# Keeping the late modes' rows twice, so that one 128-column stationary serves both row halves of a batch

## The chip, the cores and the metric

One core of a Trainium2 chip. The metric is device time in microseconds (us) of that core, as the median of several executions. Executions of one kernel mostly agree within 0.3%, so a change of 1 us needs many of them. In the profiles PE is the matmul engine, PEld its weight loads (the weights of a matmul are its stationary operand), DVE, ACT and POOL are the vector, scalar and GpSimd engines, and SP issues the stores.

## The reference

```python
def _attn_ref(q, k, v):                       # q, k, v: 8 x 8 x 576 x 64
    q_p, k_p = phi(q), phi(k)                 # phi(x) = elu(x) + 1
    kv  = einsum('bhsd,bhse->bhde', k_p, v)
    z   = sum(k_p, axis=2)
    num = einsum('bhsd,bhde->bhse', q_p, kv)
    return num / (einsum('bhsd,bhd->bhs', q_p, z)[..., None] + 1e-6)

def _moe_ref(x, w_r, w_i, w_ch):              # x: 8 x 576 x 512, 64 modes
    X = rfft(x, axis=1)[:, :64]
    Y = X * (w_r + 1j * w_i)                  # a 512 x 512 product for each mode
    u = x + irfft(Y, n=576, axis=1)
    return u + maximum(u @ w_ch, 0.0)
```

The weights of the 64 modes, 134 MB as float32, are read once.

## The kernel before

After attention and the forward transform the kernel walks over 32 pairs of modes. For each pair it loads the weights (two buffers), makes the product P, evicts it and turns it with `picks`. Work of other stages is handed out in slots between the pairs, and filler matmuls (`keep_warm`, tile zl) hold PE's clock.

```python
    def mode_pair(p):
        w = w_get(p)                           # waits for the weights of pair p
        ...                                    # 16 matmuls into P
        st = evacuate(p, P)
        work_slot(p, "mid")
        picks(2 * p, st, 2)
        if p % 4 == 3:
            ...                                # modes from 32 on:
            pin(nc.vector.tensor_copy(out=YL[:, :, :, g, :], in_=mode_rows(yt_ps)))
        work_slot(p, "end")
        keep_warm(FILL.get(p, 0))
```

The form stage, in the slots after pairs 27 to 30, makes two things from the late modes' rows of each batch b: `z`, the rows times w_ch, and `yp`, the rows transposed. Both are wanted twice, in partitions 0 to 63 and 64 to 127, for the inverse transform of the two row halves in the tail.

```python
    def form_z(b):
        z_ps = bank(f"z{b}")
        for ec in range(NDC):                  # NDC = 4
            yt = YL[:, ec].rearrange("p k g b -> p (k g) b")[:, :, b]    # 64 columns
            for h in range(2):
                pin(nc.tensor.matmul(z_ps[HALVES[h], :], yt, wch16[:, ec, :], ...))
        pin(nc.scalar.copy(out=YZ[b][:, 1, :], in_=z_ps))
    # form_y: the same with nc.tensor.transpose(y_ps[HALVES[h], ec, :], yt, id16)
```

Behind the last weights comes a tail of about 33 us: the last modes, then for each pair of row tiles six or more matmuls into `acc`, ReLU on ACT, the addition on DVE and a store of 512 KB to HBM (the first eight stores are of single tiles, 256 KB).

Of the kernel before, what the change touches and what calls it, by code (L numbers as in the profile page):

```python
# [11 lines left out]
F16 = mybir.dt.float16  # L12
# [31 lines left out]
def kernel(  # L44
# [10 lines left out]
    nc = tc.nc  # L55

    B, H, S, Dh = q.shape
# [3 lines left out]
    NDC = D // 128  # L61
# [5 lines left out]
    NL = 8  # L67
    NE = NM - NL
    NF = NM // 2
# [8 lines left out]
    xpool = ctx.enter_context(tc.tile_pool(name="xpool", bufs=1, side="right"))  # L78
    wpool = ctx.enter_context(tc.tile_pool(name="wpool", bufs=1, side="right"))

    id16 = const.tile([128, 128], F16, name="id16")
    fwd_sb = const.tile([128, 5, 2 * NM], F16, name="fwd_sb")
    pick_sb = const.tile([128, 32], F16, name="pick_sb")
    wch16 = const.tile([128, NDC, D], F16, name="wch16")
# [13 lines left out]

    QW = 4 * NJ * NP
    q_tile = lambda name: xpool.tile([128, QW], F16, tag="qTE", bufs=B, name=name)  # L100
    kv_all = [xpool.tile([128, 2, 2, 65], F16, tag="kv", bufs=B, name=f"kv{b}") for b in range(B)]
    rd_all = [xpool.tile([128, 5, 2, 4], F32, tag="rd", bufs=B, name=f"rd{b}") for b in range(B)]

    W_KEEP = 2
    pin = tc.keep_in_program_order
    PIECES = (slice(0, 2), slice(2, 4), slice(4, 6), slice(6, 7), slice(7, 8))
    HALVES = [slice(0, 64), slice(64, 128)]

    LAST = NM // 2 - 1
# [297 lines left out]
    def w_get(p: int):  # L407
        if p not in w_in and p == LAST:
            w_load_last(wpool, "w", W_KEEP)
        elif p not in w_in:  # L410
            for half in range(2):
                w_load(p, half, wpool, "w", W_KEEP)
        return w_in[p]

    def keep_warm(n: int):

        for _ in range(n):
            pin(nc.tensor.matmul(last_ps[0], id16, wch16[:, 0, :]))  # L418
# [4 lines left out]
    def work_slot(p: int, name: str):  # L423
        for _ in range(slots.get((p, name), 0)):
            if work:
                work.pop(0)()

    def product(P, x, n: int, w, dc: int, n_dc: int):
        c = dc % NDC * 32
        pin(  # L430
            nc.tensor.matmul(  # L431
                P[c : c + n, :], x, w[:, dc, :],
                start=(dc < NDC), stop=(dc >= n_dc - NDC), tile_position=(0, c),
                skip_group_check=True,
            )
        )

    def set_diagonal(p: int):
        for h in range(2):
            src = xt_v[HALVES[h], :, :, :, p].rearrange("p c t b -> p c (t b)")  # L440
            pin(nc.vector.tensor_copy(out=xz[p % 2][HALVES[h], :, h, :], in_=src))  # L441

    def evacuate(p: int, P):
        st = ystage.tile([128, D], F16, tag="ystage", bufs=2, name=f"ys{p}")
        if p % 2 == 0:
            pin(nc.vector.tensor_copy(out=st, in_=P))  # L446
        else:
            pin(nc.scalar.copy(out=st, in_=P))  # L448
        return st

    def picks(kk: int, st, n: int):
        for ec in range(NDC):
            pin(
                nc.tensor.matmul(  # L454
                    yt_ps[:, ec, kk % 8 : kk % 8 + n, :].rearrange("p m n -> p (m n)"),
                    st[:, ec * 128 : ec * 128 + 128],
                    pick_sb[:, 0 : n * 2 * B],
                )
            )

    def mode_pair(p: int):
        nonlocal yt_ps
        w = w_get(p)
        if p % 4 == 0:
            yt_ps = psW.tile([128, NDC, 8, 2 * B], F32, tag="yt", bufs=1, name=f"yt{p // 4}")
        P = psW.tile([128, D], F32, tag="P", bufs=2, name=f"P{p}")
        for dc in range(NDW):
            product(P, xz[p % 2][:, dc].rearrange("p h n -> p (h n)"), 32, w, dc, NDW)
        if p + 1 < LAST:
            set_diagonal(p + 1)  # L470
# [4 lines that stand above are left out]
            kk = 2 * p + 1  # L475
            if kk < NF:
                pin(nc.vector.tensor_copy(out=YE_T[:, :, kk - 7 : kk + 1, :], in_=yt_ps))
            else:
                g = (kk - NF) // NL + 1
                pin(nc.vector.tensor_copy(out=YL[:, :, :, g, :], in_=mode_rows(yt_ps)))  # L480
        work_slot(p, "end")
        keep_warm(FILL.get(p, 0))

# [47 lines left out]


    n_early = n_keep + n_pre
    FILL = {**{p: 7 for p in range(18, 27)}, 27: 9, 28: 5, 29: 6, 30: 4}
    ystage = ctx.enter_context(tc.tile_pool(name="ystage", bufs=1, side="right"))
    inv_sb = ystage.tile([2 * NM, S], F16, name="inv_sb")
    inv2_sb = ystage.tile([128, S], F16, name="inv2_sb")
# [1 line left out]
    lead_sb = [ystage.tile([128, S], F16, name=f"lead{b}_sb") for b in range(N_LEAD)]  # L539
    nc.sync.dma_start(out=inv_sb, in_=inv_dr.ap())  # L540
    YE_T = ystage.tile([128, NDC, NF, 2 * B], F16, name="YE_T")
    YL = ystage.tile([128, NDC, 2 * NL, NF // NL, B], F16, name="YL")
    Y8 = ystage.tile([128, NDC, NL, 2 * B], F16, name="Y8")
    nc.vector.memset(YL[:, :, :, 0, :], 0.0)

    def mode_rows(ps):
        return ps.rearrange("p c m (t b) -> p c (m t) b", b=B)

    yt_ps = None
# [5 lines left out]
    for p in range(n_early):  # L555
        mode_pair(p)
# [14 lines left out]
    def x_of(t: int):  # L571
        if t < B * NJJ:
            return x_main[t // NJJ][:, t % NJJ, :]
        i = t - B * NJJ
        return x_tail[i // 2][:, i % 2, :]
# [10 lines left out]
    def bank(name: str, shape=(128, D), dtype=F32):  # L586
        return psB.tile(list(shape), dtype, tag="bank", bufs=4, name=name)
# [115 lines left out]
    def form_z(b: int):  # L703

        z_ps = bank(f"z{b}")
        for ec in range(NDC):
            yt = YL[:, ec].rearrange("p k g b -> p (k g) b")[:, :, b]
            for h in range(2):
                pin(
                    nc.tensor.matmul(  # L710
                        z_ps[HALVES[h], :], yt, wch16[:, ec, :],
                        start=(ec == 0), stop=(ec == NDC - 1), skip_group_check=True,
                    )
                )
        pin(nc.scalar.copy(out=YZ[b][:, 1, :], in_=z_ps))

    def form_y(b: int):

        y_ps = bank(f"yp{b}", [128, NDC, 128], F16)
        for ec in range(NDC):  # L720
            yt = YL[:, ec].rearrange("p k g b -> p (k g) b")[:, :, b]
            for h in range(2):
                pin(nc.tensor.transpose(y_ps[HALVES[h], ec, :], yt, id16))
        pin(nc.vector.tensor_copy(out=YZ[b][:, 0, :], in_=y_ps.rearrange("p c r -> p (c r)")))

    def fold_lead(t: int):
# [35 lines left out]
    for b in range(B):  # L762
        pairs += [(b * NJJ, b * NJJ + 1), (b * NJJ + 2, b * NJJ + 3)]
        if b % 4 == 3:
            k = b // 4
# [82 lines left out]
    for b in range(B):  # L848
        work.append(lambda b=b: form_z(b))
        work.append(lambda b=b: form_y(b))  # L850
        if b < N_LEAD:
            work += [lambda t=t: fold_lead(t) for t in range(b * NJJ, b * NJJ + NJJ)]
    n_form = len(work) - n_fold
    first_fold, first_form = NF // 2 - 1, NE // 2 - 1
    fold_pairs = first_form - first_fold

    def share(n_items: int, steps: list):
# [10 lines left out]
    )  # L868
    share(
        n_form,  # L870
        [((first_form, "end"), 6)]
        + [((p, h), 4) for p in range(first_form + 1, LAST - 1) for h in ("mid", "end")]
        + [((LAST - 1, "mid"), 2), ((LAST - 1, "end"), 1)],
    )

    def first_rows(n: int):
# [18 lines left out]
    for p in range(n_early, LAST):  # L895
        mode_pair(p)
# [6 lines left out]
    for n in range(N_PRE):  # L903
# [6 lines left out]
    y_ps = [  # L910
        psW.tile([128, NDC, 128], F16, tag="P", bufs=2, name=f"ypl{h}")[:, 0 : NDC // 2] for h in range(2)
    ]
    y0 = psW.tile([128, D], F32, tag="P", bufs=2, name="y0l")
    last_ps.append(z1_ps.rearrange("p c m n -> p (c m n)"))
    rows = [Y8[:, ec].rearrange("p m n -> p (m n)") for ec in range(NDC)]
# [6 lines left out]
    for h in range(2):  # L922
        for ec in range(NDC):
# [3 lines left out]
                    start=(ec == 0), stop=(ec == NDC - 1),  # L927
# [5 lines left out]
    for h, eng in enumerate((nc.sync, nc.gpsimd)):  # L933
        eng.dma_start(
            out=YZ_all[64 * h : 64 * h + 64 : NF // NL].rearrange("r b z d -> r b (z d)"),
            in_=last.rearrange("p z d -> p (z d)"),
# [15 lines left out]
    def sums_of(n: int, i: int):  # L952
# [8 lines left out]
            out=x_of(0), in0=accs[0][:, 0], scalar=0.0, in1=x_of(0), op0=ALU.max, op1=ALU.add  # L961
# [50 lines left out]
```

## Time and profile before

| | before |
|---|---|
| time, median of 6 | 421.37 us (421.16 to 421.89) |
| span of the profiled execution | 419.6 us |
| PE, DVE, ACT busy | 69%, 54%, 37% of the span |
| the chain's last wait for weights ends | 386.75 us |
| last store issued by | 414.7 us |

In the page's rows of slices each digit is a tenth; in the chain of work the columns are start, duration and what it was; in the table of windows they are named in its first line.

### The profile page before, as it was taken

To read this page: it belongs to the slowest core of one execution; us is meant where nothing else is said; L and a number is where in the kernel's file an instruction comes from. 1 tells how busy PE (TensorE), PEld (TensorE's weight loads), DVE (VectorE), ACT (ScalarE), POOL (GpSimd) and SP (SyncE) were. 2 spreads that over 40 slices of the span, in tenths; PEclk is the share of its full clock that TensorE was granted. 3 is DMA by queue.
4 is the path that set the end of the run, shared out by engine and by line. 5 is a ranking of instruction groups with operands and counts; after the bars stand their busy time and mean duration, and the time that the engine had idled before them with its cause. 6 is when DMAs were issued, how large, how long until landed. Compare 5 with 4: busy or idle time off the path is not lost.

```text
span 419.6 us, 7400 instructions
## 1 busy us (share of the span) xinstructions
PE 288.7 (69%) x3115; PEld 155.9 (37%) x3115; DVE 228.6 (54%) x499; ACT 154.2 (37%) x253; POOL 58.1 (14%) x100
## 2 busy tenths in 40 slices
PE   0359799899517553444343685998798878899993
PEld 0247677787301221222121232433343324354421
DVE  4587979994404462464645353454455433512794
ACT  4677888954101011000000233344253422230782
POOL 4222224210001111111111111111111111130000
PEclk9999958989655555555555589799899989999997
DMA  8999999999999999999999999999999999998698
GB/s 219 211 212 216 210 221 206 229 206 222 222 217 212 213 223 211 216 222 209 220 220 205 225 220 205 225 215 209 224 217 208 225 216 209 223 205 162 230 395 328
DMA packets 17073, 93.17 MB, mean 222 GB/s; under 512 B 2112, under 2 KB 3024, under 8 KB 12880
## 3 DMA queue, kind: packets, MB, share of 16 engines
q0 software_dynamic: 12496, 81.48, 93.3%
q1 hardware_dynamic: 4544, 11.22, 7.2%
q8 instruction: 24, 0.39, 0.3%
q14 instruction: 9, 0.07, 0.0%
HBM read 163.93 MB, written 9.44 MB: 413 GB/s over the span
## 4 chain that ended last, share of the span: by engine, by line
DMA 65%; PE 19%; DVE 5%; issue 3%; ACT 3%; POOL 2%; DVEq 0%; ACTq 0%; POOLq 0%
DMA w<-in_moe_w_i_dram 52%; DMA pick_sb<-row_pick 8%; PE P L431 7%; DMA k<-in_k_dram 5%; PE acc L747 3%; PE acc L787 2%; PE kvp L256 2%; ACT ke L207 2%; POOL w L116 2%; PE eps L688 1%; DVE x L292 1%; DVE ke L220 1%; POOL w L128 1%; DVE k L214 1%; PE zl L418 0%
## 5 line engine op out<-in xcount | busy, mean ns | idle before, releaser
L431 PE MATMUL P<-w,xz 128*32 128x512 bf16 x496 | 48.3, 530 | 64.3 <-DMA w<-in_moe_w_i_dram 61.8
L448 ACT CAST ys<-P 128x512 f16<-128x512 f32 x15 | 8.8, 585 | 131.6 <-PE P L431 131.6
L116 POOL DMA_DIRECT2D w<-in_moe_w_r_dram x31 | 17.8, 575 | 244.2 <-PE P L431 240.7
L431 PEld LDWEIGHTS <-xz 128*32 128x32 bf16 x496 | 13.2, 115 | 85.5 <-DMA w<-in_moe_w_i_dram 56.9
L446 DVE CAST ys<-P 128x512 f16<-128x512 f32 x17 | 11.8, 691 | 53.5 <-PE P L431 53.5
L688 PE MATMUL eps<-wch,xTw 128*128 128x512 f16 x144 | 40.6, 409 | 0.0
L162 PEld LDWEIGHTS <-qT 64*128 64x128 f16 (+1 forms) x640 | 22.8, 124 | 31.7 <-issue 17.2
L671 ACT CAST x16w<-x_main 128x512 f16<-128x512 f32 x32 | 19.8, 618 | 37.7 <-DVE x_main L669 37.7
L669 DVE TENSOR_TENSOR x_main<-ya,x_main 128x512 f32<-128x512 f32 x32 | 22.0, 691 | 18.7 <-PE ya L665 18.5
L256 PE MATMUL kvp<-vpad,ke 32*128 32x130 f16 x576 | 23.3, 255 | 9.1 <-ACT qT L243 6.4
L441 DVE COPY xz<-xt_c 64x256 bf16<-64x256 bf16 x62 | 22.9, 370 | 12.1 <-PE P L431 11.3
L696 ACT CAST E<-eps 128x512 f16<-128x512 f32 (+1 forms) x40 | 21.2, 539 | 19.5 <-PE eps L688 19.5
L256 PEld LDWEIGHTS <-ke 32*128 32x128 f16 x576 | 21.4, 113 | 10.8 <-issue 8.9
L162 PE MATMUL nw<-kv,qT 64*128 64x65 f16 (+1 forms) x320 | 18.9, 240 | 9.5 <-DVE x_tail L632 4.5
L418 PE MATMUL zl<-wch,id 128*128 128x512 f16 x93 | 23.0, 380 | 0.0
L292 DVE TENSOR_TENSOR x<-num,rd 128x512 f16<-128x512 f32 x32 | 22.1, 692 | 1.1
L236 PE MATMUL qTp<-id,qe 128*128 128x128 f16 x144 | 14.3, 278 | 11.7 <-DVE qe L220 9.5
L632 DVE TENSOR_TENSOR x_main<-nw,rd 128x256 f32<-128x256 f32 x32 | 11.2, 417 | 17.3 <-PE nw L162 17.3
L207 ACT ACTIVATE qe<-q 128x1152 f16<-128x1152 f16 (+1 forms) x16 | 17.9, 1157 | 7.5 <-DMA q<-in_q_dram 7.4
L454 PE MATMUL yt<-pick_sb,ys 128*128 128x32 f16 (+1 forms) x128 | 8.8, 186 | 16.9 <-DMA pick_sb<-row_pick 10.7
L680 DVE COPY xTw<-xTp 128x512 f16<-128x512 f16 x36 | 15.0, 416 | 10.0 <-PE xTp L678 9.9
L243 ACT COPY qT<-qTp 128x1152 f16<-128x1152 f16 x16 | 19.6, 1291 | 0.5 <-PE qTp L236 0.2
(118 smaller groups left out, 494.6 us busy)
## 6 DMA issues: line engine op xcount, KB each, us to landing
w<-in_moe_w_r_dram POOLq DMA_DIRECT2D x31, 1024.0 KB, 12.5
w<-in_moe_w_i_dram POOLq DMA_DIRECT2D x31, 1024.0 KB, 16.7
out_dram<-x_main SPq DMA_DIRECT2D x12, 512.0 KB, 3.8
k<-in_k_dram POOLq DMA_DIRECT2D x8, 576.0 KB, 13.1
v<-in_v_dram POOLq DMA_DIRECT2D x8, 576.0 KB, 14.4
q<-in_q_dram POOLq DMA_DIRECT2D x7, 576.0 KB, 12.8
out_dram<-x_main SPq DMA_DIRECT2D x8, 256.0 KB, 3.8
q<-in_q_dram SPq DMA_DIRECT2D x2, 576.0 KB, 4.5
```

What stands on the lines that cost most here:

```text
L116: nc.gpsimd.dma_start(out=w_in[p][half::2], in_=two.rearrange("g (r dc) e -> (g r) dc e", dc=NDW))
L162: mm = nc.tensor.matmul(num[hpo][orow, c0 : c0 + 65], qT[rows, hpp, h2, cols], kv_sb[rows, hpp, h2, :])
L207: pin(nc.scalar.activation(out=ev[:, c], in_=heads(nm, b, c), func=AF.Exp))
L256: nc.tensor.matmul(kv_ps[:, h2, 0:130], phi["k", b][r0 : r0 + 32, j // NJ, j % NJ].rearrange("p o d -> p (o d)"), vp[r0 : r0 + 32, :, j, 0 ...
L292: nc.vector.tensor_tensor(out=dst.rearrange("p (o c d) -> p o c d", o=2, c=4), in0=nv[:, :, :, 0:64], in1=rden.unsqueeze(3).broadcast_to([ ...
L418: pin(nc.tensor.matmul(last_ps[0], id16, wch16[:, 0, :]))
L431: nc.tensor.matmul(P[c : c + n, :], x, w[:, dc, :], start=(dc < NDC), stop=(dc >= n_dc - NDC), tile_position=(0, c), skip_group_check=True,)
L441: pin(nc.vector.tensor_copy(out=xz[p % 2][HALVES[h], :, h, :], in_=src))
L669: pin(nc.vector.tensor_tensor(out=x, in0=acc, in1=x, op=ALU.add))
L671: pin(nc.scalar.copy(out=x16w[t], in_=x))
L688: nc.tensor.matmul(e_ps, xT[:, c, :], wch16[:, c, :], start=(c == 0), stop=(c == NDC - 1))
L696: pin(nc.scalar.copy(out=dst, in_=e_ps[:, cols]))
```

## The change

The rows of the late modes are kept twice side by side, so that a single 128-column stationary writes both halves at once: eight matmuls become four, in z and in yp. The second copy takes the room of kv, which for that becomes one tile. The 24 items of the form stage are handed out sooner, so that pair 30 has none, and filler takes the room.

```diff
-    kv_all = [xpool.tile([128, 2, 2, 65], F16, tag="kv", bufs=B, name=f"kv{b}") for b in range(B)]
+    kv_sb = xpool.tile([128, B, 2, 2, 65], F16, tag="kv", bufs=1, name="kv_sb")
+    kv_all = [kv_sb[:, b] for b in range(B)]
@@
-                pin(nc.vector.tensor_copy(out=YL[:, :, :, g, :], in_=mode_rows(yt_ps)))
+                late_modes(g, yt_ps)      # two tiles YL0, YL1; 2 casts into each
@@
-    FILL = {**{p: 7 for p in range(18, 27)}, 27: 9, 28: 5, 29: 6, 30: 4}
+    FILL = {**{p: 7 for p in range(18, 27)}, 27: 7, 28: 10, 29: 12, 30: 10}
@@ (form_z; form_y in the same way)
-            for h in range(2):
-                pin(nc.tensor.matmul(z_ps[HALVES[h], :], yt, wch16[:, ec, :], ...))
+            pin(nc.tensor.matmul(z_ps, late_rows(ec, b), wch16[:, ec, :], ...))
@@ (share of the form stage's items)
-        [((first_form, "end"), 6)]
+        [((first_form, "end"), 8)]
         + [((p, h), 4) for p in range(first_form + 1, LAST - 1) for h in ("mid", "end")]
-        + [((LAST - 1, "mid"), 2), ((LAST - 1, "end"), 1)],
+        + [((LAST - 1, "mid"), 0), ((LAST - 1, "end"), 0)],
```

(`late_modes` makes YL1, clears two slots of zeros and casts; `late_rows` picks the 128 columns.)

More of the change, by code (lines that the diff above doesn't have):

```diff
@@ L541, with late_modes, late_rows @@
     YE_T = ystage.tile([128, NDC, NF, 2 * B], F16, name="YE_T")
-    YL = ystage.tile([128, NDC, 2 * NL, NF // NL, B], F16, name="YL")
+    YL = [ystage.tile([128, NDC // 2, 2, 2 * NL, NF // NL, B], F16, name="YL0")]
     Y8 = ystage.tile([128, NDC, NL, 2 * B], F16, name="Y8")
-    nc.vector.memset(YL[:, :, :, 0, :], 0.0)
+    def late_modes(g: int, ps):
+        if len(YL) == 1:
+            YL.append(
+                xpool.tile([128, NDC // 2, 2, 2 * NL, NF // NL, B], F16, tag="kv", bufs=1, name="YL1")
+            )
+            for yl in YL:
+                pin(nc.vector.memset(yl[:, :, :, :, 0, :], 0.0))
+        for h, yl in enumerate(YL):
+            rows = mode_rows(ps)[:, h * (NDC // 2) : h * (NDC // 2) + NDC // 2]
+            for d in range(2):
+                pin(nc.vector.tensor_copy(out=yl[:, :, d, :, g, :], in_=rows))
+    def late_rows(ec: int, b: int):
+        yl = YL[ec // (NDC // 2)][:, ec % (NDC // 2)]
+        return yl.rearrange("p d k g b -> p (d k g) b")[:, :, b]
     def mode_rows(ps):
@@ L706, in form_z @@
         for ec in range(NDC):
-            yt = YL[:, ec].rearrange("p k g b -> p (k g) b")[:, :, b]
-            for h in range(2):
-                pin(
-                    nc.tensor.matmul(
-                        z_ps[HALVES[h], :], yt, wch16[:, ec, :],
-                        start=(ec == 0), stop=(ec == NDC - 1), skip_group_check=True,
-                    )
+            pin(
+                nc.tensor.matmul(
+                    z_ps, late_rows(ec, b), wch16[:, ec, :], start=(ec == 0), stop=(ec == NDC - 1)
                 )
+            )
         pin(nc.scalar.copy(out=YZ[b][:, 1, :], in_=z_ps))
@@ L720, in form_y @@
         for ec in range(NDC):
-            yt = YL[:, ec].rearrange("p k g b -> p (k g) b")[:, :, b]
-            for h in range(2):
-                pin(nc.tensor.transpose(y_ps[HALVES[h], ec, :], yt, id16))
+            pin(nc.tensor.transpose(y_ps[:, ec, :], late_rows(ec, b), id16))
         pin(nc.vector.tensor_copy(out=YZ[b][:, 0, :], in_=y_ps.rearrange("p c r -> p (c r)")))
```

## The prediction

> **What bounds the kernel now.** I read the page's 40 slices first, then the chain of work that ended last, then a table of windows over the last 80 us, and last the timeline around the stage that is changed. Of the slices, three rows:
>
> ```profile
> PE   0359799899517553444343685998798878899993
> ...
> PEclk9999958989655555555555589799899989999997
> DMA  8999999999999999999999999999999999998698
> ```
>
> The transfers fill 90% or more of every slice but the first and three of the last four. PE is at 7 to 9 tenths too from slice 25 on (262 us), but part of that is filler: matmuls kept only to hold its clock, on tile zl. The chain says which of the two sets the time:
>
> ```profile
> 349.86 1.01 PE P L431 x16
> 350.87 0.29 issue
> 351.16 0.54 POOL w L116
> 351.69 16.66 DMA w<-in_moe_w_i_dram
> 368.39 1.08 PE P L431 x16
> 369.47 0.29 issue
> 369.76 2.15 POOL w L128 x4
> 371.91 14.79 DMA w<-in_moe_w_i_dram
> 386.75 0.36 PE y_last L512 x8
> ```
>
> Weights come in pairs of modes, into two buffers. The product P of pair 27 (349.86) frees a buffer, the load of pair 29 is issued, lands before 368.39, and so on to 386.75. One hop covers two pairs, 368.39 - 349.86 = 18.5 us (19.4 us in undisturbed hops, such as 173.21 to 192.63), so one load takes 9.7 us. While pair 29's load is issued, pair 28's is still in flight (pair 28 starts at 358.69): the queue holds about 358.7 - 352.2 = 6.5 us of work when the new issues are done. A P that comes a microsecond or two late therefore delays an issue, but not the stream. This is the point on which everything hangs. The windows show how near PE is to the stream's pace:
>
> ```profile
> core 0: us, PE busy (x) PEld busy (x) DVE busy (x) ACT busy (x) POOL busy (x), PEclk, DMA share, GB/s
> ...
> 349.80:358.70 8.90, 5.72 (x53) 2.96 (x52) 3.65 (x7) 1.17 (x2) 1.09 (x2) 1.00 1.02 217
> 358.70:368.40 9.70, 9.09 (x64) 4.17 (x65) 5.25 (x9) 3.51 (x6) 1.08 (x2) 1.00 1.02 216
> 368.40:378.10 9.70, 8.42 (x91) 5.90 (x91) 1.70 (x4) 2.93 (x5) 3.82 (x7) 1.00 0.96 203
> 378.10:386.70 8.60, 8.26 (x79) 3.92 (x79) 3.12 (x7) 0.58 (x1) 0.54 (x1) 1.00 0.90 179
> 386.70:400.00 13.30, 12.89 (x87) 5.63 (x87) 9.31 (x14) 8.95 (x18) 0.56 (x1) 1.00 0.66 224
> 400.00:413.00 13.00, 12.45 (x69) 3.15 (x68) 12.87 (x12) 11.12 (x21) 0.00 (x0) 1.00 1.02 402
> ```
>
> The form stage lies in the first four windows, all with transfers at 0.90 to 1.02 of full. After 386.7 follows a tail of about 33 us (inverse transform, ReLU, stores), in which no instruction is changed; its PE runs at the full clock (1.00). So the change can move the end in two ways only: by moving the landing of the last weights, or by moving the clock or the start of the tail.
>
> **What the Trainium skill says.** (1) "TensorE: Matmul & The Clock Gate", Part 3 (small-M matmuls): matmuls whose outputs lie in different column groups run beside each other. The trace agrees: each row of z is made by two 64-column matmuls, and eight of them, 379 ns each, take 1.14 us together, not the 1.7 us of eight in series. (2) "TensorEngine Tiling (Array Packing)", Restrictions: column tiling switches the fast weight load off. Agrees: a 128x64 load for yp has a median of 214 ns, a 128x128 load for xTp 98 ns. (3) "VectorE: DVE Perf Modes", Mode 2x_2P: a PSUM source has one read port, so there is no doubled rate. Agrees: the 128x512 cast to YL takes 691 ns; at the page's 0.96 GHz 512 elements are 533 ns, which leaves 158 ns fixed. (4) The first page, Part 1: an idle array falls back to half clock. Agrees: the 16 products of a pair take 1.93 us at about 0.5 clock and 1.05 us at 1.00.
>
> **The change, part by part.**
>
> *z, eight batches.* Eight 64-column matmuls become four of 128 columns. The halves ran side by side already, so this is four passes of 512 rows before and after, 4 x 0.215 = 0.86 us. An eps group (four 128-column matmuls of 512) shows the same: 1.03 us from first start to last end against 1.14. I book 0.05 us a batch.
>
> *yp, eight batches.* Eight transposes with slow loads take 0.57 to 0.69 us; four 128-column ones, as in xTp, take 0.40 us. That is 0.2 to 0.3 us a batch.
>
> Together some 0.26 us a batch: pair 29's sequence z, yp repeats each 1.34 us (369.83 to 371.17), and four eps plus four xTp passes are 4 x 0.215 + 4 x 0.056 = 1.08 us. Times 8: PE gains 2.1 us, all of it inside the four windows above.
>
> *Filler.* 24 matmuls after pairs 27 to 30 become 39: +15 x 0.215 = +3.2 us. So PE is given back more than it saved.
>
> *Copies of late modes, DVE.* One cast of 0.69 us after pairs 19, 23 and 27 becomes four of 256 elements, each 0.158 + 256/0.96 ns = 0.425 us (an estimate from point 3; the 128x256 group at L632 has 417 ns). 1.70 - 0.69 = +1.0 us each time. Pair 19 gets two clears as well, about 0.27 us each (the present one was 272 ns at 110.5 us, off every path). At 19 and 23 PE afterwards waited for the weights of the next pair 0.98 and 1.72 us, so a delay of 1 to 1.6 us is at most half a microsecond of lateness for pair 20, and none for pair 24. After pair 27 the first z waits for the copies: it starts at about 353.6 in place of 352.58.
>
> *Moved items.* 24 items were split 5 after pair 27, then four blocks of about 4, then 3 in pair 30; now 8, four times 4, none. I walked the new order:
> - Pair 27: z0 at 353.6, y0 done 354.85, its copy 355.3, four folds, z1, y1 to about 357.4 (the four spare banks come free at the pace of DVE's 0.69 us adds), seven fillers of 1.5: 359.0, with the weights of 28 there at 358.6. Late by some 0.3 us.
> - Pair 28: product 1.05, four folds 3.6 (as in 362.0 to 365.97, less the picks), picks 0.3, two z and y 2.2, ten fillers 2.2: 368.4, weights at 368.4.
> - Pair 29: 1.05 + 2.2 + 0.2 + 2.2 + 2.6 = 376.7, weights at 378.1. Idle 1.4, before 1.3.
> - Pair 30: 378.1 + product 1.0 + eviction and its waits 0.9 + picks 0.2 + ten fillers 2.1 = 382.3; before, the tail's first preparatory matmul began at 382.33.
>
> So the last pair begins where it began, and its piece loads are waited for as before (386.75). *kv in one tile:* the same 4,160 bytes a partition, so no address moves; a write of the next batch stands behind the reads of the last on PE's order anyway, and the second copy takes that space after pair 19 (276 us), when the attention rows, kv's last readers, are long done (the last ran before 230 us). No cost.
>
> Sum on the path that sets the end: 0 from PE, at most 0 to 0.3 us from late issues hidden by the 6.5 us queue, 0 from the tail. Predicted 421.5 us, that is 421.46 unchanged.
>
> **The rivals.**
> - *The form stage was the bound, and ending it sooner frees the end.* For it: PE is busy 9.09 of 9.70 and 8.26 of 8.60 us there. Against: PE waited for weights before pairs 28, 29 and 30 (1.18 and 1.28 us in two of them), y_last waits 0.25 us for its piece, and the extra filler takes up the gain. If true, at most the 2.1 us saved: 419.4.
> - *The four copies become the new wait.* For it: z0 already waits 0.78 us for the one copy. Against: pair 27's own window has 8.90 - 5.72 = 3.2 us without PE work. Only if the queue ran dry would it show: 1 to 1.5 us, 422.5 to 423.
> - *The clock.* Pair 30 has no real work left in its middle, and PE pauses for the eviction. If the gate closed for one of its windows near 386 us, half clock over 3.4 us (that page's figure) costs about 1.7 us: 423. Against: pauses are 0.9 us and ten fillers follow; the throttled stretch at 339 us in the present trace shows that such a slip does happen after a 2.1 us pause.
> - *The freed PE issues the last load sooner.* Pair 31's load is issued after pair 29's product, which waits for its own weights before and after. Zero.
>
> **Range and chances.** The three times of before spread 0.6 us. A slip of the clock or a late issue adds up to 1 to 1.5 us, a start of the tail that is a little sooner takes off a few tenths. Range 420.6 to 422.4. Two per cent is 8.4 us, more than every rival together: within 2% 0.98, the other two 0.01 each.
>
> **What would show it.** Right: the chain still goes from load to load and reaches y_last at 386.5 to 387; the z group has 32 matmuls with about the old time per batch (1.0 us), yp 32 with loads near 98 ns; 12 casts to YL near 0.42 us; zl 15 higher, at 108; DMA share unchanged. Wrong: a gap in the transfers after 352 us (the queue is shallower than 6.5 us), a PEclk below 1.00 between 378 and 413 us, or y_last released by PE rather than by the load.

## The result, and the profile after

The changed kernel takes 422.23 us (median of 6, 422.04 to 422.70), the kernel before 421.37 us. Ratios here are the mean time of one kernel's fast runs over that of the other's in the same rounds, so not quite the ratio of the medians: 1.0021, 95% interval 1.0008 to 1.0034. That is the same within 2%, and within the range predicted, but it is a loss of 0.9 us clear of the noise (the slowest of the six runs before is faster than the fastest of the six changed ones), and the prediction had no term for it. The profiled spans differ by as much: 420.5 against 419.6 us.

First the rows of slices of the changed kernel:

```profile
PE   0369797999727553344343675988798877988992
...
PEclk9999989558955556555555598899899999999996
DMA  8999999999999999999999999999999999997797
```

The transfers are as full as before. The chain of work of the changed kernel:

```profile
348.95 1.07 PE P L432 x16
...
350.85 18.19 DMA w<-in_moe_w_i_dram
369.08 1.08 PE P L432 x16
...
372.60 14.14 DMA w<-in_moe_w_i_dram
386.79 0.36 PE y_last L513 x8
...
411.89 1.22 DVE x_tail L834
413.11 1.13 DVEq L1020
```

It still goes from load to load, and its last wait for weights ends at 386.79 us, 0.04 later than before. The chain of the kernel before ends so:

```profile
411.82 1.23 DVE x_tail L821
413.05 1.13 DVEq L1007
```

All compute of the tail is therefore 0.06 us later, and no more. The 0.9 us arise after the last addition, when there is nothing left but stores. The waits of the DMA-issuing queue at the end (waited for: us in total, times, longest), before and then changed:

```profile
SPq L1007 <- DMA out_dram<-x_main: 2.3, 2, 1.2
```

```profile
SPq L1020 <- DMA out_dram<-x_main: 3.2, 3, 1.2
```

The end waits 0.9 us longer for the landing of output, three times in place of two. From the DMA view of the last microseconds, 418.2 to 421 us, again before and changed:

```profile
DMA packets 0, 0.00 MB, mean 0 GB/s; under 512 B 0, under 2 KB 0, under 8 KB 0
```

```profile
DMA packets 6, 0.02 MB, mean 7 GB/s; under 512 B 1, under 2 KB 1, under 8 KB 6
```

In the changed kernel six packets are still going out, when in the kernel before all are done. The packet records show the last ones of 4,096 bytes one behind the other, 0.155 us each, the last ending at 418.99 us against 418.09 before: they look like one DMA engine that is behind the other fifteen. (The records do not name the engine; this is inferred.)

What could hold back a single engine? The DMA view has a queue q8 of instructions, 24 packets of 16 KB in either kernel. In the window 390 to 400 us of the kernel before, and 400 to 412 us of the changed one:

```profile
q1 hardware_dynamic: 1361, 2.64, 74.4%
...
q8 instruction: 1, 0.02, 0.6%
```

```profile
q1 hardware_dynamic: 1437, 4.78, 100.7%
q8 instruction: 1, 0.02, 0.6%
```

(Columns: packets, MB, share of 16 engines.) The last 16 KB of instructions are fetched at 396.4 us before and at 406.2 us in the changed kernel, and each takes about 1.05 us of an engine. The 74% is a mean: the stores begin at 391.7 us, fill the engines around 396 too (101.4% from 395.5 to 397.5), and leave a little room soon after (92.4% from 397 to 400); from 400 to 412 there is none (101.5% before, 100.7% changed).

That the fetch holds up the stores is seen in how long they take to land. The stores issued from 398 to 404 us and from 404 to 408 us (count, size, median us from issue to landing), before and then changed:

```profile
out_dram<-x_main SPq DMA_DIRECT2D x4, 512.0 KB, 3.6
...
out_dram<-x_main SPq DMA_DIRECT2D x3, 512.0 KB, 3.8
```

```profile
out_dram<-x_main SPq DMA_DIRECT2D x4, 512.0 KB, 3.0
...
out_dram<-x_main SPq DMA_DIRECT2D x3, 512.0 KB, 4.9
```

In the changed kernel landing steps up from 3.2 to 4.85 us with the store issued at 404.6 us, which is in flight at the fetch, and stays there to the last store (5.05; before 4.2).

The Trainium skill has the reason for the move: "Runtime: NRT & Kernel Launch", Instruction fetch mechanics, says that an engine's instructions come in blocks of 16 KiB, 256 instructions, over a DMA queue of its own. The trace agrees on the size. Between the first and the last of the 24 fetches of the kernel before, PE went through 2,914 weight loads and as many matmuls, some 253 instructions to a fetch, so these are PE's instructions. The profile has 6,230 of them before and 6,132 after: 64 less in z, 64 less in yp (matmul and weight load each), 30 more of filler. PE therefore reaches the block's boundary 98 instructions later. In the tail it runs some 310 matmuls and weight loads in 26.3 us (386.7 to 413), so 98 of them are about 8 us; measured, the fetch moved by 9.8.

### The profile page after: what moved, and what is told of

Same layout as the page of the kernel before. It is cut to its first block, busy times and chain, and to the rows that moved or that the text cites. A ratio compares the mean times of both kernels' runs of the same rounds, so it can differ in the third digit from the quotient of the medians.

```text
span 420.5 us, 7312 instructions
## 1 busy us (share of the span) xinstructions
PE 289.5 (69%) x3066; PEld 156.2 (37%) x3066; DVE 230.8 (55%) x509; ACT 154.0 (37%) x253; POOL 57.9 (14%) x100
## 4 chain that ended last, share of the span: by engine, by line
DMA 68%; PE 18%; DVE 4%; issue 3%; POOL 3%; ACT 2%; DVEq 0%; ACTq 0%; POOLq 0%
DMA w<-in_moe_w_i_dram 53%; DMA pick_sb<-row_pick 8%; PE P L432 7%; DMA k<-in_k_dram 7%; PE acc L760 3%; PE acc L800 2%; POOL w L117 2%; DVE x L293 1%; PE kvp L257 1%; PE eps L706 1%; ACT ke L208 1%; PE ya L683 1%; PE xTp L696 1%; POOL w L129 1%; PE zl L419 0%
## 5 line engine op out<-in xcount | busy, mean ns | idle before, releaser
L432 PEld LDWEIGHTS <-xz 128*32 128x32 bf16 x496 | 13.2, 114 | 86.5 <-DMA w<-in_moe_w_i_dram 57.9
L706 PE MATMUL eps<-wch,xTw 128*128 128x512 f16 x144 | 39.0, 397 | 0.0
L163 PEld LDWEIGHTS <-qT 64*128 64x128 f16 (+1 forms) x640 | 23.0, 124 | 32.0 <-issue 16.8
L687 DVE TENSOR_TENSOR x_main<-ya,x_main 128x512 f32<-128x512 f32 x32 | 22.0, 689 | 16.8 <-PE ya L683 16.6
L257 PE MATMUL kvp<-vpad,ke 32*128 32x130 f16 x576 | 24.6, 266 | 8.9 <-ACT qT L244 6.0
L257 PEld LDWEIGHTS <-ke 32*128 32x128 f16 x576 | 22.6, 118 | 10.5 <-issue 8.1
L419 PE MATMUL zl<-wch,id 128*128 128x512 f16 x108 | 26.2, 380 | 0.0
L163 PE MATMUL nw<-kv_sb,qT 64*128 64x65 f16 (+1 forms) x320 | 18.9, 241 | 9.5 <-DVE x_tail L650 4.5
L163 PE MATMUL num<-kv_sb,qT 64*128 64x65 f16 (+1 forms) x320 | 16.5, 220 | 5.6 <-DVE x L293 3.6
```

Source lines behind the costliest of these rows:

```text
L163: mm = nc.tensor.matmul(num[hpo][orow, c0 : c0 + 65], qT[rows, hpp, h2, cols], kv_sb[rows, hpp, h2, :])
L257: nc.tensor.matmul(kv_ps[:, h2, 0:130], phi["k", b][r0 : r0 + 32, j // NJ, j % NJ].rearrange("p o d -> p (o d)"), vp[r0 : r0 + 32, :, j, 0 ...
L419: pin(nc.tensor.matmul(last_ps[0], id16, wch16[:, 0, :]))
L432: nc.tensor.matmul(P[c : c + n, :], x, w[:, dc, :], start=(dc < NDC), stop=(dc >= n_dc - NDC), tile_position=(0, c), skip_group_check=True,)
L687: pin(nc.vector.tensor_tensor(out=x, in0=acc, in1=x, op=ALU.add))
L706: nc.tensor.matmul(e_ps, xT[:, c, :], wch16[:, c, :], start=(c == 0), stop=(c == NDC - 1))
```

## The experiments

Theory F: the loss is that fetch, now among stores that leave no room for it. Theory S, the rival: the form stage, its copies or its filler cost the time, by some way that the chain does not show.

The handle for all of them is a number of tiny matmuls (16 columns, two PE instructions each) in pairs 5 to 14, where PE is less than half busy and the weights set the pace. They shift the place of the later fetches without touching the stages in question.

```diff
         keep_warm(FILL.get(p, 0))
+        for _ in range(PADS.get(p, 0)):       # spread evenly over pairs 5 to 14
+            pin(nc.tensor.matmul(last_ps[0][:, 0:16], id16, wch16[:, 0, 0:16]))
```

All kernels gave correct results. Runs of the kernel before: 421.37 us (median of 11) for the first four, 421.44 us (11) for the next four, 421.82 us (9) for the last three.

### The changed kernel with its 98 instructions given back (49 pads)

> The changed kernel with 49 tiny matmuls (98 PE instructions, as many as the change took away) added in pairs 5 to 14, where PE is half idle. Theory F (the 0.9 us comes from a 16 KB fetch of PE instructions that now falls among the output stores): the last fetch goes back from 406 us to about 396 us and the time to 421.4 us (ratio to before 0.999 to 1.001). Theory S (the form stage, its copies or its filler cost the 0.9 us): 422.2 us, ratio 1.002, as without the pads.

Measured 421.46 us, ratio 0.9995 (0.9977 to 1.0013). The DMA view from 390 to 400 us, and then from 418.2 us on:

```profile
q8 instruction: 1, 0.02, 0.7%
```

```profile
DMA packets 0, 0.00 MB, mean 0 GB/s; under 512 B 0, under 2 KB 0, under 8 KB 0
```

The fetch is back at 396.6 us, the late packets are gone, and so is the loss, with the whole change still in. Theory S falls for this.

### The kernel before, with the fetch moved to the bad place (79 pads)

> The kernel before with 79 tiny matmuls (158 PE instructions; with fetches of 256 instructions this puts the last one where the changed kernel has it). Theory F: last fetch at about 406 us, time about 422.2 us, ratio 1.002, though nothing of the change is in it. Theory S: 421.4 us, ratio 1.000.

Measured 422.37 us, ratio 1.0016 (0.9998 to 1.0033; one long run of the kernel before, 423.91, widens it and pulls the ratio down. The six runs of this kernel, 422.02 to 422.51, lie above ten of the eleven of before, which end at 421.85). The window from 418.2 us on:

```profile
DMA packets 8, 0.02 MB, mean 7 GB/s; under 512 B 3, under 2 KB 3, under 8 KB 8
```

Nothing of the change is in this kernel, and it has a loss of the same size and the same late packets; its fetch is at 406.4 us. In its profiled execution only 0.6 us of the loss arise after the last addition (0.8 in the changed kernel); the additions themselves end 0.3 us later than before, in an execution with a stretch at half clock from 364.5 to 371.3 us.

### The fetch later still (53 pads), and earlier (25 pads)

> The kernel before with 53 tiny matmuls (106 PE instructions): two fetches near the tail, at about 387 and 410 us. Theory F: the later the fetch among the stores, the less its DMA engine can catch up: 422.2 to 422.5 us, ratio 1.002 to 1.003. Theory S: 421.4 us.

Measured 422.39 us, ratio 1.0026 (1.0000 to 1.0052, with one run at 425.15). Fetch at 411.5 us, last store packet at 419.14. The landing of stores steps up with the one issued at 409.3 us, from 4.0 to 5.3 us.

> The kernel before with 25 tiny matmuls (50 PE instructions): the last fetch moves from 396 to about 391 us, where the stores have hardly begun, and the next would fall past the end. Theory F: at most the time of before, 421.0 to 421.4 us, ratio 0.999 to 1.000. Theory S, or pads that cost time by themselves: 421.4 us or more.

Measured 421.35 us, ratio 0.9992 (0.9972 to 1.0012). Fetch at 391.1 us. So pads as such cost nothing, and being earlier than 396 gains nothing.

### The place between (105 pads)

> The kernel before with 105 tiny matmuls (210 PE instructions): last fetch at about 401 us, between that of before (396, no cost) and of the changed kernel (406, +0.9 us). Theory F with catching up (an engine that fetched early makes it good while the stores are not yet backed up): in between, 421.6 to 422.1 us. Theory F without catching up (any fetch after 393 us costs the same): 421.4 us is excluded by the kernel before, so this would read 422.2 us only if the limit lies before 401.

Measured 421.77 us (421.67 to 422.17), ratio 1.0002 (0.9989 to 1.0014). The trace has what was expected, a fetch at 400.9 and a last packet at 418.51 us, halfway between 418.09 and 418.99. Landing steps up with the store issued at 399.6 us, from 2.9 to 4.3 us. The time is where it should be as well, but it is not resolved: the kernel before itself ran in two groups, 421.3 to 421.8 and 422.2 to 422.6 us, for a reason that I have no trace of.

### The changed kernel with the fetch at the best place (74 pads)

> The changed kernel with 74 tiny matmuls (148 PE instructions): last fetch at about 391 us, before the stores are backed up, and no later one. Theory F: 421.2 to 421.5 us, ratio to before 0.999 to 1.001; it is the best place found for the fetch, so if the changed form stage gained anything it would show here as less than 421.2.

Measured 421.35 us (421.26 to 421.45), ratio 0.9990 (0.9976 to 1.0003). With the fetch out of the way at 391.3 us, the change neither costs nor gains. (The ratio is drawn down by the two groups of the kernel before; its medians in the other two calls are 421.37 and 421.44.)

The traces resolve what the times do not. From the end of the last addition to the end of the span pass 5.2 to 5.5 us in the nine profiled executions whose last fetch begins 16.8 us or more before that end, those with more filler below among them; 5.9 us with 105 pads (13.2 us before it), 6.0 and 6.2 us with 79 pads and in the changed kernel (8 us), 6.6 us with 53 pads (2.5 us). The later the fetch, the larger the loss.

### The two halves of the change, each alone

Rows kept twice, with the old split and filler, 64 pads:

```diff
-    FILL = {..., 27: 7, 28: 10, 29: 12, 30: 10}
+    FILL = {..., 27: 9, 28: 5, 29: 6, 30: 4}
     (and the split 6, 4 x 4, 2, 1 of before)
```

> The rows kept twice and the 128-row stationaries alone, with the split of items and the filler of before, and 64 tiny matmuls in pairs 5 to 14 to keep the number of PE instructions (fetch at 396 us). Theory F: the gain of some 2 us of PE is hidden behind the weights: 421.4 us, ratio 0.999 to 1.001. Theory S: the copies cost something, 421.8 to 422.2 us. If the form stage bounded the kernel: 419.4 us.

Measured 421.49 us, ratio 0.9997 (0.9979 to 1.0015): no gain, no loss.

The new split and filler on the old stationaries, 113 pads:

> The kernel before with the new split of items and the new filler alone (30 PE instructions more), and 113 tiny matmuls: 256 more in all, fetch at 396 us. Theory F: hidden, 421.4 us, ratio 0.999 to 1.001, although PE has more to do here than in either kernel. Theory S: products 28 to 30 come late and the time is 421.8 us or more.

Measured 422.69 us (421.30 to 424.02), ratio 1.0022 (0.9998 to 1.0046). A miss, and of another kind: the executions differ by 2.7 us, and in the profiled one y_last begins at 388.60 in place of 386.75 us. The table of windows shows more:

```profile
349.80:386.70 36.90, 34.10 (x276) 18.24 (x268) 12.29 (x25) 8.21 (x14) 6.54 (x12) 0.91 1.00 206
```

PEclk is 0.91 over 36.9 us: 6.8 us, from 354.5 to 361.3, are at half clock, and from 349 us on the chain is PE's work, with short steps of ACT and DVE, to the end. The same stretch is in the profiles of the two copies alone and of the changed kernel with 49 and 74 pads (6.8 us between 353 and 361), and costs nothing there: PE had idle time left to absorb it, which this kernel has not. That the longer executions are those with such a stretch is likely, but only one has a trace.

### How late may PE be? 10, 20 and 45 more filler matmuls after pair 27

These are the kernel before, with pads to make 256 PE instructions more in all, so that the fetch stays at the same place in the program. The edit for 20:

```diff
-    FILL = {..., 27: 9, 28: 5, 29: 6, 30: 4}
+    FILL = {..., 27: 29, 28: 5, 29: 6, 30: 4}
```

> The kernel before with 20 more filler matmuls after pair 27 (4.3 us at 0.215 us each) and 108 tiny ones in pairs 5 to 14, 256 PE instructions in all, so that the fetch stays at 396 us. It tests the prediction's central step: product 28 is some 3.1 us late, but the queue of 6.5 us hides it. By the prediction: time 421.4 us, ratio 0.999 to 1.001, last weights still used at 386.5 to 387 us. If the form stage bounds the kernel (or the queue is shallow): 424 us or more.

Measured 423.64 us (421.51 to 424.94), ratio 1.0034 (1.0007 to 1.0062).

> The same with 45 more filler matmuls (9.7 us), 83 tiny ones, again 256 PE instructions. Product 28 is some 8.5 us late, which is more than the 6.5 us that the queue holds: the transfers should show a gap after 368 us and the end should move by 2 to 3.5 us, 423.5 to 425 us. If the time stays at 421.4 the queue is deeper than I reckoned; if it moves by 8 us or more there is no queue to speak of.

Measured 428.03 us (426.61 to 430.16), ratio 1.0156 (1.0126 to 1.0186). Both miss. From the chain of the kernel with 20 more:

```profile
331.39 17.46 DMA w<-in_moe_w_i_dram
348.90 1.07 PE P L431 x16
...
356.06 7.56 PE zl L418 x29
...
389.34 0.39 PE y_last L514 x16
```

From 349 us on the chain has no load in it any more: it is PE's work, with short steps of ACT and DVE between, up to the end. The transfers did not run dry with 20 (share 0.98 of the engines between 349.8 and 386.7 us); with 45 they did in part (0.81). What is used up is PE's own idle time in the stage: in the kernel before its matmuls waited for weights 1.18, 0.09 and 1.28 us before pairs 28, 29 and 30 and 0.25 us before y_last, 2.8 us together. (The expectation of the next run says 3.1 to 3.3; that takes for pair 29 the 0.59 us of the weight load.) 20 fillers are 4.3 us, 1.5 too many, 45 are 9.7 us, 6.9 too many; the medians rose by 2.2 and 6.6.

The clock has a part in this. Both profiled executions have 6.8 us at half clock (from 351.6 and from 354.1 us), which cost 2.2 us with 20 (29 fillers took 7.56 us for 6.2, eight z 1.99 for 1.14) and 2.6 us with 45 (54 fillers took 14.26 us for 11.6). With 20 that makes 1.5 + 2.2, less the 0.9 us by which pair 27 began sooner: 2.8 us; in the chains y_last is 2.6 us late. With 45 it makes 9.5, and y_last is 9.2 us late. The fastest execution with 20, 421.51 us, is no slower than the kernel before, so where the limit lies between 2.15 and 9.7 us is not sharp.

> The kernel before with 10 more filler matmuls after pair 27 (2.15 us) and 118 tiny ones (256 PE instructions in all). After the runs with 20 and 45 more I hold PE's own idle time between 349.8 and 386.7 us, some 3.1 to 3.3 us, for the slack, not the queue of loads. Then 2.15 us fit, unless the clock falls to half for one window, which takes 1.7 us more: most executions 421.4, some up to 422.3 us, median 421.4 to 421.9. If there is no slack: 423.5 us.

Measured 421.23 us (421.13 to 421.52), ratio 0.9988 (0.9975 to 1.0000). 2.15 us fit into the 2.8. (This call is the one with the two groups of the kernel before, so the ratio below 1 is no gain.)

## Why the prediction was right or wrong, point by point

**The bound: right.** The weights' stream sets the pace to 386.8 us in both kernels, and the form stage's gain on PE is hidden (the two copies alone: 421.49 us).

**Its reason: wrong.** The prediction said that everything hangs on the 6.5 us of loads in the queue. The queue does keep the stream going, but lateness of PE is passed from pair to pair to the tail, and is made good only by PE's idle time, 2.8 us. The runs with 20 and 45 more fillers showed it. The predicted result held because the change adds less than that: 3.2 us of filler less 2.1 us saved. That it fits the range is luck in one respect: the upper end, 422.4, was set for a slip of the clock or a late issue, and neither is in the profile.

**z and yp: right in size.** From the changed kernel's timeline (start, duration, then engine and line; the bracket is the idle time before it):

```profile
350.99 1.42 DVE L557 CAST YL<-yt 128x256 f16<-128x256 f32 x4 [4.77 <-PE yt L455]
...
351.81 0.43 PE L726 MATMUL z<-wch,YL 128*128 128x512 f16 x1 [0.85 <-DVE YL L557]
...
370.06 1.08 PE L726 MATMUL z<-wch,YL 128*128 128x512 f16 x4
...
370.98 0.41 PE L736 MATMUL yp<-id,YL 128*128 128x128 f16 x4
...
371.17 0.64 PEld L726 LDWEIGHTS <-YL 128*128 128x128 f16 x4
...
371.23 1.03 PE L726 MATMUL z<-wch,YL 128*128 128x512 f16 x4
```

Four wide matmuls of z take 1.03 to 1.08 us (eight narrow ones took 1.14), yp 0.41 (expected 0.40), and a batch repeats after 371.17 - 370.06 = 1.11 us (between the starts of the weight loads, which at 370.06 coincides with the matmul's; expected 1.08, before 1.34). The one miss is the weight load: 147 ns, expected near 98. The 128 columns of the late rows lie eight elements apart, those of xTp one; the load is faster than the narrow one's 214 ns, but not at the contiguous one's time. The narrow columns lay eight apart too, so the prediction put the whole of 214 against 98 ns down to column tiling, while the spacing may have a part in it. The load lies beside the matmuls and cost nothing.

**The copies: each right, their cost too high.** Twelve casts of 416 ns median (expected 425). But z starts 1.12 us after the picks (350.69 to 351.81) against 1.05 before, not a microsecond later: its first two matmuls read YL0 alone, which is ready after two casts. The other two wait 0.46 us more.

**The walk: right, in part by luck.** Pair 28 was expected at 359.0, it ran at 358.74; pair 29 at 368.4, it ran at 369.08 and had waited 1.05 us for weights; pair 30 at 378.1 (378.20); the tail's first preparation at 382.3 (382.32). But the walk had PE 0.3 us late for pair 28, and PE waited 0.84 us for its weights: pair 27 had begun at 348.95 and not at 349.79, in an execution without the stretch at half clock that the kernel before has at 339.5 us. The table of windows of the changed kernel has the clock at 1.00 from 349.8 to 413 us, as expected.

```profile
368.40:378.10 9.70, 8.38 (x64) 4.91 (x64) 1.70 (x4) 2.93 (x5) 3.82 (x7) 1.00 0.97 205
378.10:386.70 8.60, 7.34 (x61) 2.70 (x61) 2.35 (x5) 0.00 (x0) 0.55 (x1) 1.00 0.90 178
```

In pair 30 PE is busy 7.34 us, before 8.26.

**The tail: here the sum failed.** The step was "0 from the tail", for the reason that no instruction in it is changed. None is, but their place in the program is: 98 instructions fewer ahead of it put the last 16 KB fetch 9.8 us later, where the delay of the stores stays to the end. Of the 0.90 us between the profiled executions 0.84 arise after the last addition, and the loss can be put into the kernel before (421.4 to 422.4) and taken out of the changed one (422.2 to 421.4 or 421.5) by nothing but the number of PE instructions.

**The rivals.** The form stage as bound would have given 419.4 us: excluded. The copies as a new wait: excluded by the two copies alone. The clock: no dip in the changed kernel's profile, but nine of the thirteen profiles have one of 6.8 us between 351 and 372 us, longer than the prediction reckoned and earlier. (All nine are of kernels with pads; whether the pads bring it is open.) In the changed kernel with 49 pads pair 28 comes 2.5 us later with it (361.27 against 358.74), and y_last only 0.2; with the new filler on the old stationaries PE could not absorb it. Put together: the two copies make the room that the filler takes.

**What stays open.** That the late packets and the fetch share one engine is inferred from their order and from the numbers, not read off a record; the steps in landing, 0.8 to 1.6 us, are not quite the 0.9 to 1.1 us of a fetch. An instruction queue of 8 KB packets (q14, 0.3 to 0.65 us each) also fetches twice in the tail of every kernel; its part is not separated. Why a fetch at 391 or 396 us costs nothing is not shown either: in every run landing grows to 4.0 us or more by the last store. Why the kernel before at times runs at 422.2 to 422.6 us, or at 423 to 424, is not known; none of those executions has a trace. No version that was run is clear of the kernel before: the best medians, 421.23 and 421.35, lie within its spread.

## What to carry to other kernels

When a change takes instructions away, the rest of the program moves against its 16 KB fetches, and in a stage that saturates the DMA engines one of them can cost about a microsecond, as here; before crediting or blaming a change of that size, shift the program by a few idle instructions and measure again. Where the chain ran through transfers, the slack of PE was its own idle time up to the end, not the depth of the queue of loads: add filler to measure it, and look at the clock of the profiled execution before reading the result. And two 64-column matmuls that already ran beside each other left little to gain from one of 128 (1.14 us for four pairs, 1.03 to 1.08 for four wide ones).

## What the Trainium skill lacked or had wrong

- "Runtime: NRT & Kernel Launch", Instruction fetch mechanics, calls the cost of crossing a block's boundary mostly hidden. It is hidden for PE (its last matmul ends 0.06 us later), but the last fetch took 0.9 to 1.1 us (once 1.5), by inference of one of the DMA engines that the kernel's own transfers use, and among saturated stores that cost 0.9 to 1.0 us at the end (422.2 to 422.4 against 421.4 us); some 17 us or more before the end of the additions it cost nothing measurable.
- "TensorE: Matmul & The Clock Gate", Weight-path perf modes, names packed and strided columns alike for the fast weight load, without a difference in time; nor does the general note on strided reads in "SBUF — State Buffer" put a time on it. Here 128 fp16 columns eight elements apart took 147 ns (median in yp; 144 in z), contiguous ones 98 ns.
- No page says how much a late PE may lag behind a stream of loads. Here 2.15 us fitted in all five executions and 4.3 us in one of six, with 2.8 us of idle time on PE and some 6.5 us of loads queued; the profiled execution with 4.3 had a stretch at half clock besides.
